# Two attention heads interleaved in hand order: the next head's K work inside the present head's V and gradient work, side work dealt out in slots

## The chip, the cores and the metric

The kernel runs on one core of a Trainium2 chip. The metric is the device time of one execution, in microseconds (us). Several executions are timed, and runs of a changed kernel are timed next to runs of the kernel before on the same chip. The profile is one execution recorded by the hardware; its span is some 2 us shorter than the time on the metric.

Names of engines: PE is TensorE, the matrix engine (PEld is its loading of weights, which overlaps its products: 385.3 and 337.2 us busy in a span of 565.1). DVE is VectorE, ACT is ScalarE, POOL is GpSimd (here it issues stores), SP is SyncE (here it issues loads). In the timelines below each engine starts its instructions in program order, even where a later one is what another engine waits for (DVE runs w_sb and half of dV before pj while PE stands for pj 1.93 us).

## The reference, cut to what matters

The kernel computes a forward pass and all its gradients: one decoding step of attention (32 heads, 4096 cached keys and values each, head width 128) mixed by a gate with a small MLP.

```python
def _A_ref(x, k_cache, v_cache, wq, wo):           # x: one row of 640
    q = (x @ wq) -> 32 heads of 128
    scores = einsum("bhqd,bhkd->bhqk", q, k_cache) * 128 ** -0.5
    p = softmax(scores)
    o = einsum("bhqk,bhkd->bhqd", p, v_cache)
    return o -> one row of 4096 @ wo
def _B_ref(x, w1, b1, w2): ...                     # Mish MLP, 640 -> 1728 -> 640
out = g * a + (1 - g) * b                          # g = sigmoid((x * gate_w).sum())
# returned: out and, by vjp, the gradients of x, k_cache, v_cache, wq, wo, w1, b1, w2, gate_w
```

The large data are K and V (32 MiB each, read) and dK and dV (32 MiB each, written). For one head, with dO the gradient that arrives at o: dP = V dO, ds = p * (dP - sum(p * dP)), dV = p (outer) dO, dK = ds (outer) q, dq = ds K. All of it is matrix times vector: K and V are transposed on PE only to be multiplied by one vector (in the kernel before the transposes are 223.3 of PE's 385.3 busy us).

## The kernel before: the parts that matter

A head is four functions, called one after the other. Two pieces of a head are used throughout this text: a *chunk* is four 128x128 f32 transposes on PE (two bf16 columns are moved as one f32) and an ACT copy of the result out of PSUM; the *products* of a chunk are eight small matrix products with it.

```python
tr_ps bufs=3; sa_ps bufs=2; sb_ps bufs=2; gr_ps bufs=1      # 3 + 2 + 2 + 1: eight PSUM banks in use
def transposes(src, c): ...   # 4 x nc.tensor.transpose(f32), then nc.scalar.copy  ("chunk")
def products(out, tb, c, vec): ...                            # 8 small matmuls

def head_k(h):                       # scores
    for c in range(NT):              # NT = 4 chunks
        ts.append(transposes(kts[h], c))
        if c: products(S, ts[c - 1], c - 1, ...)
    products(S, ts[NT - 1], NT - 1, ...)
    nc.vector.reduce_max(m32[:], S, axis=AX.X)
def head_v(h):                       # V chunks 0..3 with dP = V dO; between them:
    ...                              # MM: transpose of the maximum -> negM -> e = exp(S - max)
    ...                              # Z: sum of e over partitions -> zs -> rz = 1/zs -> p_bf
def head_o(h):
    outer(dV, st["p"], row, 0, J // 2)                        # DVE, half of dV
    nc.vector.scalar_tensor_tensor(pj[:], in0=DP, ..., accum_out=part[:])
    outer(dV, st["p"], row, J // 2, J)
    for j in range(J): nc.tensor.matmul(O, ...)               # 32 one-column products
    nc.tensor.transpose(PT, part[:]...)                       # PE waits for pj
    ...                                                       # dd, ds, o_all on DVE
def head_d(h):
    for j in range(J): nc.tensor.matmul(DQ, ..., rhs=st["ds"]...)   # PE waits for ds
    outer(dK, ...); nc.scalar.copy(dq_all...); outer(dK, ...)

for h in range(H):
    load_k(h + 3); load_v(h + 3)
    if hh == 2: q += prep_steps(g + 1); load_wo(g + 2); ...   # groups of G = 4 heads
    head_k(h); head_v(h)
    if h > 0: side(q if q and hh > 1 else mq, 1)              # one step of side work
    head_o(h)
    side(q if q and hh > 1 else mq, 1)
    head_d(h)
    if hh == G - 1: q += finish_steps(g)
    side(q if q else mq, 1)
    if hh == G - 2 or g == NG - 1: side(q, 4)                 # a block of four steps
```

"Side work" is the MLP, the preparation of the next group of four heads (its q and dO vectors, from wq and wo) and the finishing of the last group (its part of the output, dwo, dx). A step of it may be several large DVE instructions with a PE product in between.

## Time and profile before

| | before |
|---|---|
| time, median | 566.4 us |
| PE, DVE, ACT busy, share of the span | 68%, 56%, 33% |
| a head, from one score maximum to the next | 16.5 us mean, 13.1 to 25.4 |
| full-clock share of that time | 35% |
| bytes moved, mean rate | 165 MB, 292 GB/s |

The first lines are the page of the profile: the span, the busy times, and of the 40 equal slices the rows of PE, of the clock that PE was granted (tenths of full speed) and of DMA (busy share in tenths), then the engines' shares of the chain of waits that ended last.

```profile
span 565.1 us, 13730 instructions
PE 385.3 (68%) x5916; PEld 337.2 (60%) x5916; DVE 313.6 (56%) x780; ACT 188.2 (33%) x410; POOL 46.4 (8%) x95
...
PE   2899776786668735787667655678668755777840
...
PEclk9956556777777757777757666566677776577655
DMA  7995796699779976698784998669878975763493
...
PE 45%; DVE 36%; ACT 7%; issue 6%; DMA 4%; SPq 1%; ACTq 0%; DVEq 0%
```

No engine is full, PE alternates between full and half-empty slices, and the chain changes hands between PE and DVE. The table of waits says on what (total us, how often, longest):

```profile
DVE m L502 <- PE sA L481: 129.8, 31, 13.6
...
DVE zs L525 <- PE sA L522: 44.6, 32, 1.7
...
PE sB L577 <- DVE ds_bf L565: 36.7, 31, 1.4
...
PE sB L560 <- DVE pj L554: 29.9, 31, 2.0
```

DVE waits for scores (m is the score maximum), PE waits for DVE's gradients (pj, ds). One such place in the timeline (start us, duration us, instruction, in brackets the idle time of the engine before it and what ended it):

```profile
313.57 0.94 PE L559 MATMUL sA<-e_bf,Vn 128*128 128x1 bf16 x32
...
314.47 0.67 DVE L453 TENSOR_SCALAR w_sb<-dh_bc,cols_f 128x1728 bf16<-128x1728 bf16 x1
315.06 1.22 DVE L536 TENSOR_TENSOR dV_sb<-p_bf,qd 128x2048 bf16<-128x2048 bf16 x1
...
316.19 0.18 DVE L554 SCALAR_TENSOR_TENSOR pj<-sB,e_bf 128x32 f32<-128x32 f32 x1
...
316.44 0.48 PE L560 MATMUL sB<-ident_f,part 128*128 128x128 f32 x1 [1.93 <-DVE pj L554]
```

PE has finished the products of this head and stands for 1.93 us, because DVE first does side work (w_sb) and half of dV and only then pj.

The last view of the kernel before is the clock. It is cut into windows of 3.41 us (bounds set on the changes of the clock in the trace: in this trace the clock stands at 0.5 or 1.0, for 3.413 us or a whole multiple of it, up to the last record) and shows only the instructions of the tile `tr`, the f32 transposes; the number in brackets after PE counts those that touch the window, and PEclk is the granted clock in it.

```profile
427.50:430.92 3.42, 1.18 (x8) 0.72 (x8) 1.35 (x3) 1.00 0.95 395
430.92:434.33 3.41, 0.08 (x1) 0.11 (x2) 0.00 (x0) 0.50 0.27 111
434.33:437.74 3.41, 3.30 (x14) 2.54 (x15) 1.47 (x3) 0.50 1.00 336
437.74:441.16 3.42, 2.07 (x16) 1.52 (x14) 2.00 (x4) 1.00 0.99 304
441.16:444.57 3.41, 0.84 (x6) 0.42 (x4) 1.17 (x2) 1.00 1.01 420
444.57:447.98 3.41, 0.57 (x3) 0.67 (x4) 0.00 (x0) 0.50 0.97 396
```

A window with 14 transposes at half clock is followed by one at full clock, that one (16) by another, and the one with 6 by a fall. At half clock one transpose starts 213 ns after the other (median over the trace), at full clock 109 ns.

### The profile page before, as it was taken

To read this page: it belongs to the slowest core of one execution; us is meant where nothing else is said; L and a number is where in the kernel's file an instruction comes from. 1 tells how busy PE (TensorE), PEld (TensorE's weight loads), DVE (VectorE), ACT (ScalarE), POOL (GpSimd) and SP (SyncE) were. 2 spreads that over 40 slices of the span, in tenths; PEclk is the share of its full clock that TensorE was granted. 3 is DMA by queue.
4 is the path that set the end of the run, shared out by engine and by line. 5 is a ranking of instruction groups with operands and counts; after the bars stand their busy time and mean duration, and the time that the engine had idled before them with its cause. 6 is when DMAs were issued, how large, how long until landed. Compare 5 with 4: busy or idle time off the path is not lost.

```text
span 565.1 us, 13730 instructions
## 1 busy us (share of the span) xinstructions
PE 385.3 (68%) x5916; PEld 337.2 (60%) x5916; DVE 313.6 (56%) x780; ACT 188.2 (33%) x410; POOL 46.4 (8%) x95
## 2 busy tenths in 40 slices
PE   2899776786668735787667655678668755777840
PEld 1798765675557634676556645677556644666730
DVE  4221655666556775566449673454645483456574
ACT  2403332343333313353423323334334423334310
POOL 0000000010001000010001100010001000010210
PEclk9956556777777757777757666566677776577655
DMA  7995796699779976698784998669878975763493
GB/s 293 419 382 248 283 377 238 231 382 360 315 243 345 383 275 242 228 373 352 277 297 176 365 381 317 235 230 337 320 280 297 360 300 170 246 248 141 176 403 148
DMA packets 26328, 164.93 MB, mean 292 GB/s; under 512 B 2812, under 2 KB 2812, under 8 KB 10012
## 3 DMA queue, kind: packets, MB, share of 16 engines
q1 hardware_dynamic: 14156, 82.03, 40.3%
q0 software_dynamic: 12112, 82.03, 37.3%
q8 instruction: 46, 0.75, 0.5%
q14 instruction: 14, 0.11, 0.1%
HBM read 82.03 MB, written 82.03 MB: 290 GB/s over the span
## 4 chain that ended last, share of the span: by engine, by line
PE 45%; DVE 36%; ACT 7%; issue 6%; DMA 4%; SPq 1%; ACTq 0%; DVEq 0%
PE tr L472 30%; DVE dV_sb L536 13%; ACT tT L474 6%; DVE dK_sb L536 6%; PE sA L481 4%; DMA w_sb<-in_B_w_dram 4%; DVE junk L253 4%; DVE junk L330 4%; PE h_ps L353 3%; PE sB L577 3%; PE sB L481 2%; DVE junk L414 2%; DVE dj L563 2%; DVE junk L450 1%; DVE ds_bf L565 1%
## 5 line engine op out<-in xcount | busy, mean ns | idle before, releaser
L474 ACT COPY tT<-tr 128x512 f32<-128x512 f32 x256 | 149.0, 586 | 152.9 <-PE tr L472 142.5
L472 PE MATMUL tr<-ident_f,Kn 128*128 128x128 f32 x512 | 127.9, 416 | 0.0
L481 PEld LDWEIGHTS <-tT 128*128 128x128 bf16 x2048 | 82.2, 103 | 65.5 <-ACT tT L474 58.9
L472 PE MATMUL tr<-ident_f,Vn 128*128 128x128 f32 x512 | 95.4, 320 | 0.0
L472 PEld LDWEIGHTS tr<-ident_f,Kn 128*128 128x128 f32 x512 | 94.3, 217 | 1.7 <-issue 1.6
L536 DVE TENSOR_TENSOR dV_sb<-p_bf,qd 128x2048 bf16<-128x2048 bf16 x64 | 78.1, 1221 | 18.5 <-ACT p_bf L530 18.5
L502 DVE TENSOR_REDUCE m<-sA 128x1 f32<-128x32 f32 x32 | 6.1, 192 | 129.8 <-PE sA L481 129.8
L536 DVE TENSOR_TENSOR dK_sb<-ds_bf,qd 128x2048 bf16<-128x2048 bf16 x64 | 75.3, 1217 | 0.0
L472 PEld LDWEIGHTS tr<-ident_f,Vn 128*128 128x128 f32 x512 | 67.3, 164 | 0.0
L577 PEld LDWEIGHTS <-Kn 128*128 128x128 bf16 x1024 | 34.7, 107 | 43.6 <-issue 43.6
L481 PE MATMUL sA<-qd,tT 128*128 128x2 bf16 x1024 | 48.1, 168 | 16.3 <-ACT tT L474 16.1
L481 PE MATMUL sB<-qd,tT 128*128 128x2 bf16 x1024 | 45.4, 165 | 17.7 <-ACT tT L474 17.7
L577 PE MATMUL sB<-ds_bf,Kn 128*128 128x1 bf16 x1024 | 31.8, 165 | 36.7 <-DVE ds_bf L565 36.7
L579 ACT CAST dq_all<-sB 128x1 bf16<-128x1 f32 x32 | 5.2, 162 | 132.5 <-PE sB L577 132.5
L557 POOL DMA_DIRECT2D out_dram<-dV_sb x32 | 17.2, 537 | 374.8 <-DVE dj L563 374.8
L560 PE MATMUL sB<-ident_f,part 128*128 128x128 f32 x32 | 13.8, 431 | 30.0 <-DVE pj L554 29.9
L525 DVE TENSOR_REDUCE zs<-sA 128x1 f32<-128x32 f32 x32 | 6.1, 192 | 44.6 <-PE sA L522 44.6
L559 PE MATMUL sA<-e_bf,Vn 128*128 128x1 bf16 x1024 | 30.2, 163 | 0.0
L253 DVE SCALAR_TENSOR_TENSOR junk<-wo_g,da_bc 128x640 bf16<-128x640 bf16 x32 | 26.3, 822 | 4.8 <-DMA wo_g<-in_A_wo_dram 3.8
L559 PEld LDWEIGHTS <-Vn 128*128 128x128 bf16 x1024 | 28.2, 96 | 0.0
L560 PEld LDWEIGHTS sB<-ident_f,part 128*128 128x128 f32 x32 | 5.3, 167 | 32.8 <-DVE pj L554 32.8
L585 POOL DMA_DIRECT2D out_dram<-dK_sb x31 | 16.5, 532 | 102.0 <-DVE dK_sb L536 60.4
(144 smaller groups left out, 332.1 us busy)
## 6 DMA issues: line engine op xcount, KB each, us to landing
Kn<-in_A_k_cache_dram SPq DMA_DIRECT2D x32, 1024.0 KB, 10.0
Vn<-in_A_v_cache_dram SPq DMA_DIRECT2D x32, 1024.0 KB, 12.7
out_dram<-dV_sb POOLq DMA_DIRECT2D x32, 1024.0 KB, 5.0
out_dram<-dK_sb POOLq DMA_DIRECT2D x31, 1024.0 KB, 10.4
wq_g<-in_A_wq_dram SPq DMA_DIRECT2D x4, 1280.0 KB, 7.9
wo_g<-in_A_wo_dram SPq DMA_DIRECT2D x8, 640.0 KB, 13.2
out_dram<-wo_g POOLq DMA_DIRECT2D x8, 640.0 KB, 10.9
out_dram<-dwq_t POOLq DMA_DIRECT2D x5, 896.0 KB, 7.9
```

Of the source, the lines that this page charges most:

```text
L253: nc.vector.scalar_tensor_tensor(junk[:, 0:D], in0=wos[g][:, i, :], scalar=1.0, in1=da_bc[:], op0=ALU.mult, op1=ALU.mult, accum_out=gp["do ...
L330: nc.vector.scalar_tensor_tensor(junk[:], in0=wqs[w][:, rc, :], scalar=1.0, in1=dq_bc[:, w * WG * Dh:(w + 1) * WG * Dh], op0=ALU.mult, op1 ...
L353: nc.tensor.matmul(hps["t"][:, fc:fc + 1], lhsT=w1_sb[:, rc, :].rearrange("p (q c) -> p q c", c=FCN)[:, :, fc], rhs=x_bf[:, rc:rc + 1], st ...
L472: nc.tensor.transpose(tp[:, t, :], flat[:, k * P:(k + 1) * P], ident_f[:])
L474: nc.scalar.copy(sb[:].rearrange("p a b -> p (a b)"), tp[:].rearrange("p a b -> p (a b)"))
L481: nc.tensor.matmul(out[:, 2 * k:2 * k + 2], lhsT=tb[:, t, par, :], rhs=vec[:, par, :], start=(par == 0), stop=(par == 1))
L536: nc.vector.tensor_tensor(dst[:, a:b, :].rearrange("p j (a b) -> p j a b", b=2), col[:, a:b, :].unsqueeze(2).to_broadcast([P, n, Dh // 2, 2]),
L557: nc.gpsimd.dma_start(dVv[h], dV[:])
L559: nc.tensor.matmul(O, lhsT=vts[h][:, j, :], rhs=st["e"][:, j:j + 1], start=(j == 0), stop=(j == J - 1))
L560: nc.tensor.transpose(PT, part[:].to_broadcast([P, P]), ident_f[:])
L577: nc.tensor.matmul(DQ, lhsT=kts[h][:, j, :], rhs=st["ds"][:, j, 0:1], start=(j == 0), stop=(j == J - 1))
L585: nc.gpsimd.dma_start(dKv[h], dK[:])
```

## The change

Its intent: fill PE's waits with the next head's K work, fill DVE's waits with the previous head's dK, and deal the side work out evenly. It adds no arithmetic and moves no other bytes. The core of the diff:

```diff
-    sb_ps = ... bufs=2        gr_ps = ... bufs=1
+    sb_ps = ... bufs=1        gr_ps = ... bufs=2
+    def slot(h, p=2, d=1):    # deals ready items: all "T" (tiny), d of "D" (DVE), p of "P" (PE)
+        ...                   # an item is ready when its deps were dealt in an earlier slot
-    def head_k / head_v / head_o / head_d
+    def period(h):            # K chunks of h+1 live inside head h
+        nc.vector.reduce_max(m32[:], S, axis=AX.X)
+        V(0); dk_half(h - 1, 0)                    # dK of the head before, on DVE
+        V(1); ...MM...; dk_half(h - 1, 1)
+        V(2); dP(0); ...e...; V(3); dP(1); ...Z, zs, rz, p_bf...
+        dP(2); o_part(0, J); dP(3)
+        slot(h)
+        ...pj...                                   # now ahead of dV
+        dv_half(h, 0)
+        nc.tensor.transpose(PT, part...)
+        k_chunk(h + 1, 0, tk); k_chunk(h + 1, 1, tk)
+        ...dd, ds...
+        dv_half(h, 1)
+        s_chunk(h + 1, 0, tk); k_chunk(h + 1, 2, tk)
+        slot(h)
+        s_chunk(h + 1, 1, tk)
+        ...DQ: 32 one-column products...
+        k_chunk(h + 1, 3, tk); s_chunk(h + 1, 2, tk)
+        ...dq copy...
+        s_chunk(h + 1, 3, tk)
+        slot(h)
     for h in range(H):
-        if hh == 2: q += prep_steps(g + 1); load_wo(g + 2); load_wq(...)
+        if hh == 0: prep_steps(g + 1, h)           # now a period earlier: S of the next group
+        if hh == 3: load_wo(g + 2); load_wq(...)   # starts inside period 3; loads a head later
```

`k_chunk` makes a chunk of K, `s_chunk` its products (written S0 to S3 below, the chunks K0 to K3, V0 to V3). The steps of side work were cut into items, most of them of one to four DVE instructions.

## The prediction

> **What bounds the kernel now.** No engine: on the page PE is 68% busy, DVE 56%, ACT 33%, and the DMA queues take 78% of 16 engines' span. From head 0's score maximum (21.0 us, timeline) to head 31's (534.0 us) a head takes 16.5 us (13.1 to 25.4). The chain of waits alternates between PE transposes (30%) and DVE outer products and side work (dV 13%, dK 6%, wq/wo/w1 reductions some 13%), one waiting for the other. In "who waited for whom" DVE waits 129.8 us for scores and 44.6 us for the softmax sum; PE waits behind pj and ds (30 + 37 us), and at heads 11, 19, 27 some 10 us for a block of DVE side work.

> **Clock.** [...] steps of 3.41 us between 0.5 and 1.0 (mean 0.68). [...] windows full of 1-column products stay at half clock; nearly every rise follows a half-clock window with 11 to 13 of the 128x128 f32 transposes. Now K and V lie back to back (32 transposes in 8 to 10 us), which always offers such a window.

> **What the change does.** It removes no arithmetic and no bytes. It puts the next head's K chunks on PE where PE waited for pj, dd, ds; the previous head's dK on DVE where DVE waited for scores and softmax; and deals one DVE item (0.8 to 1.3 us) and up to two PE items per slot, three slots a head, so no 5 to 10 us blocks remain. One sB bank goes to side work; sB is read last by the small dq copy, so one should not stall.

> **Cost of a head after** (timeline durations). PE at half clock: 8 x 1.15 (chunk and product) + O 1.0 + DQ 1.0 + max, sum and part transposes 0.9 + S3 waiting for its copy 0.6 + side 45/32 = 1.4: 14.1; at full clock some 10 to 11 us. DVE: 2.44 + 2.35 + 2.1 small operations + 2.9 side = 9.8 us. ACT 5.9. DMA: 165 MB at 375 to 385 GB/s of its full windows = 435 us, 13.5 us a head. So PE becomes the bound, DMA close behind at about 90%.

> The interleave spreads the transposes: V in one run of 16, K broken by slots and DQ. I expect fewer windows to reach the threshold and the mean clock to *fall* to 0.55 to 0.65, giving back part of the gain: about 14.1 us a head instead of 11 to 12.

> **Sum.** 21 us start + 31 x 14.1 = 437 + 31 tail (534 to 565 before; five dx, dwo and dwq_l still follow the last head) = 489 us. Range 462 to 518. Faster by over 2%: 0.96; within 2%: 0.03; slower: 0.01.

> **What would show it.** Score maxima lie some 14 us apart, evenly; PE busy 83 to 92%, its microseconds somewhat up, clock 0.55 to 0.65; DVE busy 62 to 66%, same microseconds; mean HBM rate 330 to 345 GB/s; in the chain PE over 65%, DVE under 20%, mostly at the ends; waits for scores under 60 us.

> **What would make it wrong.** Faster (near 465): transposes still raise the clock, period near 12.5, then DMA is the floor. Slower (over 515): in-order engines bind each other (negM waits for MM behind V0, V1; pj for the last dP behind O; dV1 stands before slot work), DVE becoming co-critical; or full DMA delays output buffers and loads, showing as DMA waits in the chain.

What the Clock paragraph says is of the trace of the kernel before: from 28.2 to 38.4 us PE is busy with one-column products all the time (10.2 us) at a clock of 0.5; 30 of the 31 rises (first and last five windows left out) follow a half-clock window in which 11 to 13 transposes start, the other one with 14; and the 32 transposes of a head take 7.7 to 9.7 us and put 12 to 14 into one window in 32 of 32 heads. "The threshold" is that count: 30 of 32 half-clock windows with twelve or more are followed by full clock, 1 of 5 with ten or eleven, none of 66 with at most nine. The costs of a head are estimates from durations in the same trace (at half clock a chunk starts 1.15 us after the last, O takes 0.94 us and DQ 0.99, S3 waits 0.54 for its copy; with a transpose every 109 ns in place of 213 the same sum gives 10.8 us, the "10 to 11" at full clock), and so is the floor of DMA: stretches of 17 us with DMA 98% busy or more moved 368 to 386 GB/s.

## The result, and the profile after

The changed kernel takes 464.1 us (462.8 to 465.8, four runs) against 566.4 us. Ratios in this text are the mean time of one kernel's fast runs over the mean of the fast runs of the kernel before in the same rounds, so not quite the ratio of the medians quoted (and where two experiments ran on different chips, the ratios are what can be compared): here 0.820, with a 95% interval of 0.816 to 0.824. The result is correct.

| | before | after |
|---|---|---|
| first score maximum | 21.0 us | 20.7 us |
| a head, mean | 16.5 us | 13.1 us |
| of it PE busy / PE idle | 11.86 / 4.69 us | 11.98 / 1.14 us |
| full-clock share | 35% | 20% |
| last score maximum to the end | 31.1 us | 34.6 us |

(PE busy here is the union of products and weight loads between the first and the last score maximum, over 31 heads.) The same lines of the page as before:

```profile
span 462.1 us, 13671 instructions
PE 389.3 (84%) x5916; PEld 363.1 (79%) x5916; DVE 311.1 (67%) x785; ACT 186.3 (40%) x410; POOL 49.3 (11%) x95
...
PE   2799999999999999799988999799898999999600
...
PEclk9965555656556665687565656656656756556555
DMA  7999999958798899999999899997999999845995
...
PE 61%; DMA 18%; DVE 9%; ACT 7%; issue 2%; SPq 0%; ACTq 0%; DVEq 0%
```

PE's microseconds stayed (385 to 389), the idle time between them went. The clock row lies lower than before (mean 0.61 in place of 0.68). The table of waits, the lines that answer to those before, and two that are new:

```profile
DVE m L621 <- PE sA L559: 42.4, 24, 5.4
...
DVE zs L637 <- PE sA L635: 21.6, 29, 1.2
...
PE sB L651 <- DVE pj L648: 8.5, 16, 2.8
...
DVE junk L278 <- DMA wo_g<-in_A_wo_dram: 8.0, 3, 3.6
...
PE qc_ps L268 <- DMA wq_g<-in_A_wq_dram: 5.7, 3, 2.6
...
PE sB L670 <- DVE ds_bf L659: 1.2, 1, 1.2
```

PE's waits for pj and ds fell from 66.6 to 9.7 us. The waits for wq are new and those for wo have grown (before: one of 3.8 us, at the start), and they weigh more in the chain (DMA 18%) than their 14 us suggest, since the chain then counts the whole transfer that ended last. In the timeline such a place looks so:

```profile
294.75 1.22 DVE L574 TENSOR_TENSOR dV_sb<-p_bf,qd 128x2048 bf16<-128x2048 bf16 x1
296.32 0.61 PEld L268 LDWEIGHTS <-wq_g 128*128 128x128 bf16 x20 [2.37 <-DMA wq_g<-in_A_wq_dram]
```

The clock windows after, in the same view of `tr`:

```profile
303.04:306.46 3.42, 2.07 (x9) 1.81 (x9) 1.17 (x2) 0.50 1.00 419
306.46:309.87 3.41, 2.16 (x9) 1.39 (x8) 1.76 (x3) 0.50 0.98 394
309.87:313.28 3.41, 2.07 (x9) 1.90 (x10) 0.76 (x2) 0.50 0.73 298
313.28:316.70 3.42, 2.04 (x8) 1.25 (x8) 1.38 (x3) 0.50 0.58 230
316.70:320.11 3.41, 2.89 (x12) 2.44 (x12) 1.37 (x3) 0.50 0.98 293
320.11:323.52 3.41, 0.78 (x6) 0.56 (x6) 1.17 (x2) 1.00 0.99 378
```

Here 8 or 9 transposes lie in most windows and the clock stays at half; it rises once, after the window with 12, and the full-clock window is then spent on other work (6 transposes touch it). PE is hardly idle (0.9 us in the four windows before the one with 12): the spread of the transposes, not idleness, seems to keep the clock down. That was the forecast; the experiments test it.

### The profile page after: what moved, and what is told of

The parts are those of the page before. It is cut to its first block, busy times and chain, and to the rows that moved or that the text cites. A ratio compares the mean times of both kernels' runs of the same rounds, so it can differ in the third digit from the quotient of the medians.

```text
span 462.1 us, 13671 instructions
## 1 busy us (share of the span) xinstructions
PE 389.3 (84%) x5916; PEld 363.1 (79%) x5916; DVE 311.1 (67%) x785; ACT 186.3 (40%) x410; POOL 49.3 (11%) x95
## 4 chain that ended last, share of the span: by engine, by line
PE 61%; DMA 18%; DVE 9%; ACT 7%; issue 2%; SPq 0%; ACTq 0%; DVEq 0%
PE tr L550 35%; DMA wo_g<-in_A_wo_dram 10%; DMA wq_g<-in_A_wq_dram 8%; ACT tT L552 5%; PE sB L670 5%; PE sA L559 5%; PE h_ps L404 3%; PE sA L618 3%; PE sB L559 2%; DVE junk L375 2%; DVE junk L278 2%; PE sB L651 2%; PE sA L625 1%; DVE zs L637 1%; PE ap_ps L356 1%
## 5 line engine op out<-in xcount | busy, mean ns | idle before, releaser
L550 PE MATMUL tr<-ident_f,Kn 128*128 128x128 f32 x512 | 121.8, 400 | 0.0
L550 PE MATMUL tr<-ident_f,Vn 128*128 128x128 f32 x512 | 119.9, 396 | 0.0
L559 PEld LDWEIGHTS <-tT 128*128 128x128 bf16 x2048 | 90.1, 107 | 36.6 <-ACT tT L552 29.5
L550 PEld LDWEIGHTS tr<-ident_f,Vn 128*128 128x128 f32 x512 | 93.3, 209 | 0.0
L550 PEld LDWEIGHTS tr<-ident_f,Kn 128*128 128x128 f32 x512 | 91.7, 207 | 0.3 <-issue 0.3
L574 DVE TENSOR_TENSOR dK_sb<-ds_bf,qd 128x2048 bf16<-128x2048 bf16 x64 | 77.7, 1216 | 0.0
L618 PEld LDWEIGHTS <-Vn 128*128 128x128 bf16 x1024 | 31.2, 100 | 5.0 <-issue 5.0
L670 PEld LDWEIGHTS <-Kn 128*128 128x128 bf16 x1024 | 29.7, 103 | 2.0 <-issue 2.0
L627 DVE TENSOR_REDUCE negM<-sA 128x1 f32<-128x128 f32 x32 | 9.3, 291 | 25.6 <-PE sA L625 25.6
L375 DVE SCALAR_TENSOR_TENSOR junk<-wq_g,dq_bc 128x1024 bf16<-128x1024 bf16 x20 | 24.3, 1216 | 0.1
L637 DVE TENSOR_REDUCE zs<-sA 128x1 f32<-128x32 f32 x32 | 6.1, 192 | 21.9 <-PE sA L635 21.6
```

Source lines behind the costliest of these rows:

```text
L375: nc.vector.scalar_tensor_tensor(junk[:], in0=wqs[w][:, rc, :], scalar=1.0, in1=dq_bc[:, w * WG * Dh:(w + 1) * WG * Dh], op0=ALU.mult, op1 ...
L550: nc.tensor.transpose(tp[:, t, :], flat[:, k * P:(k + 1) * P], ident_f[:])
L559: nc.tensor.matmul(out[:, 2 * k:2 * k + 2], lhsT=tb[:, t, par, :], rhs=vec[:, par, :], start=(par == 0), stop=(par == 1))
L574: nc.vector.tensor_tensor(dst[:, a:b, :].rearrange("p j (a b) -> p j a b", b=2), col[:, a:b, :].unsqueeze(2).to_broadcast([P, n, Dh // 2, 2]),
L618: nc.tensor.matmul(O, lhsT=vts[h][:, j, :], rhs=st["e"][:, j:j + 1], start=(j == 0), stop=(j == J - 1))
L670: nc.tensor.matmul(DQ, lhsT=kts[h][:, j, :], rhs=ds[:, j, 0:1], start=(j == 0), stop=(j == J - 1))
```

## The experiments

Eleven kernels ran, in three rounds or more. Their first purpose is to divide the gain; the second, to test the clock, the DMA and the late loads.

### e1 and e2: which part made the gain

e1 keeps the even dealing and takes the interleave and the deferral of dK back:

```diff
-        V(0); dk_half(h - 1, 0) ... dk_half(h - 1, 1)
-        (K chunks of h+1 between PT and the last slot)
+        slot(h); DQ; dk_half(h, 0); dq copy; dk_half(h, 1); slot(h)
+        for c in range(NT): k_chunk(h + 1, c, tk); if c: s_chunk(h + 1, c - 1, tk)
+        s_chunk(h + 1, NT - 1, tk)
```

> Changed kernel, but the K work of the next head stands after DQ in one run and dK follows its own head, as before; side work still dealt in slots. If the even dealing is most of the gain: under 510 us, DVE waits for the scores still large. If the interleave of K is most of it: over 520 us. Clock theory (transposes in one run of 32 raise the clock): mean clock back to 0.66 or more, from 0.61; PE busy under 75%.

e2 keeps the interleaved period and takes side work, its order and the PSUM banks from the kernel before:

```diff
-        slot(h)                  # three times
+        side_at(h, 1..3)         # the side() calls of the kernel before, at the same three places
-    sb_ps bufs=1, gr_ps bufs=2
+    sb_ps bufs=2, gr_ps bufs=1
```

> The head of the changed kernel (K interleaved, dK one head later), with the side work, its order and the PSUM banks of the kernel before. If the interleave is most of the gain: under 510 us; if the dealing is: over 520 us. Heads at group ends should still be several us longer than the others (20 us or more against 12 to 13). Clock 0.58 to 0.64.

Measured: e1 513.5 us (ratio 0.907), e2 498.9 us (0.877; one of its four runs, the profiled one, is slow and left out of the ratio). e1 fell between its two alternatives, e2 within its first: by the ratios, dealing alone saves 53 us, the interleaved period alone (K's interleave and the deferral of dK, not separated here) 70 us, both together 102 us. They overlap by some 20 us, since both remove the same PE idle time: PE idles 4.69 us a head before, 2.59 in e1, 2.06 in e2 and 1.14 after. e2's heads are uneven as expected (10.3 to 23.7 us). The figures inside e2 are from its slow run, which had the clock (0.597) of a fast one that took 499.3 us.

One expectation of e1 was plainly missed: the clock did not return to 0.66, it was 0.639, although K and V lay back to back again. The trace shows how. In its later part e1's heads take 13.6 us one after the other, which is four windows of 3.41 us, so heads keep their place against the windows; in this position the run of 32 gives 8, 8 and 13 transposes, only the third raises the clock, and the window that gets it has 3 or 4. So nearly every head still wins its full-clock window, but only when its transposes are over. A long run alone is no guarantee; where it lies against the windows counts too. (PE was 77% busy, over the 75% expected.)

A kernel with the old banks in the changed kernel could not be run: a deadlock. The dealt items hold a side bank from one slot to the next (o4 is computed in one, copied in a later one), so one bank is likely too few; the second side bank seems a condition of the dealing. What it is worth by itself stays open.

### e3: the late loads

```diff
-        if hh == 0 and g + 1 < NG:
+        if hh == 1 and g + 1 < NG:      # prepare the next group one head later
```

> Changed kernel with the preparation of the next group dealt one head later, so that the wq and wo loads have a head more to land. If the late loads hold PE up as the four holes near 190, 242, 293 and 347 us suggest: 454 to 458 us, no wait on DMA for wq_g or wo_g in the table of waits after the start. If full DMA only moves the wait to other loads: 461 to 465 us.

Measured: 453.3 us (0.798; six runs, one slow and left out of the ratio), just under its first range, and the waits went as forecast. The waits of PE for wq_g fell from 5.7 to 0.8 us, after the start none for wo_g is left; idle PE fell from 1.14 to 0.88 us a head. Changing one number makes it better than the changed kernel by 11 us. Some 8 us (31 x 0.26) are PE's idle time; the rest is not divided. The profiled run of e3 is its fastest, 14.8 us below the changed kernel's, and has a clock of 0.63; over the fast runs the clock is 0.604 to 0.628, against 0.610 to 0.619 for the changed kernel, so a better clock is not shown.

### e4: is DMA close behind PE?

```diff
-            nc.gpsimd.dma_start(dVv[h], st["dV"][:])
+            nc.gpsimd.dma_start(dVv[h][:, 0:J // 2, :], st["dV"][:, 0:J // 2, :])   # wrong result
```

> Wrong result on purpose: only half of each dV is stored, 16.8 of 165 MB less. If PE bounds the heads: 2% less at most, 455 to 463 us, mostly from loads that land sooner. If DMA bounds them: 8 to 10% less, under 430 us.

Measured: 456.5 us (0.805). A tenth fewer bytes saves 1.8% (0.805 over 0.820; 1.6% by the medians), as the first alternative has it, and PE's idle time, 0.86 us a head in place of 1.14, makes as much as all of it (31 x 0.28 = 8.7 us): again the loads that land sooner. So the number of bytes does not bound the changed kernel; late loads cost it some 8 us.

### e5, e6 and e8: the clock

e5 builds on e3 and puts the K work in one piece. Nothing is added or removed:

```diff
         s_chunk(h + 1, 0, tk); k_chunk(h + 1, 2, tk)
-        slot(h)
         s_chunk(h + 1, 1, tk)
-        DQ
         k_chunk(h + 1, 3, tk); s_chunk(h + 1, 2, tk)
+        slot(h)
+        DQ
         dq copy
         s_chunk(h + 1, 3, tk)
```

> e3 with the K work in one piece: K0 K1 S0 K2 S1 K3 S2, then the slot and DQ, then S3, so that DQ and not idle PE covers S3's wait for its copy (0.6 us a head, 19 us in all), and 16 K transposes stand together. If PE alone bounds the heads: 434 to 442 us. If DMA or DVE is as close as PE: 448 us or more. Clock theory (a window needs some 12 transposes): mean clock at or above e3's 0.63.

("Some 12" is what the trace of the kernel before shows: 30 of 32 half-clock windows with twelve or more transposes are followed by full clock; over all traces, pooled below, 287 of 302, but also 54 of 164 with ten or eleven.)

Measured: 427.1 us (0.751; one slow run left out of the ratio), outside both alternatives, on the fast side. The clock is 0.72, the full-clock share of the heads 43% in place of 24%, PE busy 10.88 us a head in place of 11.87 in e3. The view of `tr`:

```profile
226.49:229.90 3.41, 3.29 (x14) 2.54 (x15) 1.46 (x3) 0.50 1.01 418
229.90:233.31 3.41, 2.10 (x16) 1.58 (x15) 1.80 (x4) 1.00 1.01 421
233.31:236.73 3.42, 0.64 (x4) 0.41 (x4) 1.24 (x3) 1.00 1.02 421
236.73:240.14 3.41, 1.14 (x6) 1.34 (x7) 0.04 (x1) 0.50 1.00 423
```

But e5 changes two things: the run of transposes, and DQ now covers S3's wait for its copy. e8 separates them. It is e5 with the 32 one-column products of O, which nothing waits for soon, moved into the K work:

```diff
-        dP(2); o_part(0, J); dP(3)
+        dP(2); dP(3)
 ...
         s_chunk(h + 1, 0, tk)
+        o_part(0, J)
         k_chunk(h + 1, 2, tk)
```

> e5 with one thing moved: the 32 one-column products of O stand between the K transposes (after S0) instead of between dP2 and dP3, so K is broken into 8 and 8 transposes, while S3's wait stays covered by DQ. If the unbroken run is what raised the clock in e5: clock back to 0.60 to 0.66, 438 to 448 us. If the covered S3 wait was the gain, or the clock follows busy PE: clock 0.70 or more, 424 to 430 us.

Measured: 449.3 us (0.794), just over its first range, with the clock in it: 0.64, full-clock share 25%. Same instructions, same cover for S3, and breaking the run of 16 into 8 and 8 costs 22 us (24 by the ratios; the two ran on different chips). In the view of `tr`:

```profile
297.43:300.85 3.42, 1.91 (x8) 1.71 (x8) 1.14 (x2) 0.50 1.00 418
300.85:304.26 3.41, 2.19 (x8) 1.43 (x8) 1.10 (x3) 0.50 1.02 426
304.26:307.67 3.41, 2.32 (x10) 2.24 (x11) 1.02 (x3) 0.50 1.02 404
307.67:311.09 3.42, 1.24 (x10) 0.87 (x9) 1.44 (x3) 1.00 0.96 393
```

But the move has a second effect: O had covered two other waits, which lie open in e8, while e5 alone waits long for wq. From the tables of waits, two lines of e8 and one of e5:

```profile
PE sB L650 <- DVE pj L647: 18.4, 29, 1.8
PE sB L559 <- ACT tT L552: 6.5, 21, 0.3
```

```profile
PE qc_ps L268 <- DMA wq_g<-in_A_wq_dram: 19.8, 3, 10.7
```

(In e5 the wait for pj is 6.8 us; in e8 that for wq is 0.7.) So the total time of e8 does not separate the two, and neither does its small distance from e3 (0.794 against 0.798, intervals that overlap). PE's busy time does, since the instructions are the same: 11.87 us a head in e3, 11.78 in e8, 10.88 in e5. What the higher clock is worth is therefore 31 x 0.90 = 28 us from e8 to e5 and 31 x 0.99 = 31 us from e3 to e5. The covered wait of S3 was worth something too (PE's waits before S products are 19.2 us in e3 and 1.9 in e5), but the wait for wq took as much back: idle PE is 0.88 us a head in e3, 0.91 in e8 and 1.09 in e5. So what e5 gains over e3 is PE's busy time at the higher clock; the idle time, taken together, rose. The rival, that the clock follows how busy PE is, falls too: PE is 86% busy in e8 at 0.64 and 83% in e5 at 0.72.

e6 goes further: DQ of a head moves into the next head's period, so that K of the next head and its V stand in one run of 32.

```diff
         dP(3)
+        dq(h - 1, A[:, 96:97])        # DQ of the head before, into a free column of this head's bank
         slot(h)
 ...
-        DQ and dq copy of h at the end of the period
-        slot(h) ... slot(h)           # the second and third slot
+        slot(h, 1) ... slot(h, 0)     # deal fewer PE items
```

> e3 with the DQ products of a head moved into the next head's period, between the last dP and the part transpose, so that the K transposes of the next head and its V transposes stand in one run of 32, as in the kernel before. Clock theory: mean clock 0.68 or more, two full-clock windows in four, PE time of a head from 11.9 to 11 us or less. If that carries through: 420 to 432 us; if DMA or DVE becomes the bound: 435 to 450 us with the clock up all the same. Rival, that the clock follows how busy PE is: the clock stays at 0.63.

Measured: 440.6 us (0.775; the profiled run is slow). The clock rose as forecast, to 0.72 to 0.73 in the three fast runs, but the time is not in the range for a gain that carries through, only in the second one (435 to 450 us), and worse than e5. DVE waits 29.3 us for the part transpose, which now stands behind DQ (22.3 us in e5, of which 10.5 are one wait for wq), and the last head has an unshared DQ at the end (40.2 us from the last score maximum to the end). Which of these costs more, or whether it is the smaller slots, was not tested, and these profile numbers are from a slow run.

Pooled over the traces of the two kernels and all eleven experiments, counting the transposes that start in each window and leaving out the first and last five windows of a trace (a few windows before the first record of the clock are taken as half): of 683 half-clock windows with at most nine, 4 are followed by full clock; of 164 with ten or eleven, 54; of 302 with twelve or more, 287. Among full-clock windows the same number divides: 110 of 114 with twelve or more keep it, 7 of 328 with at most nine. (In the traces of the two kernels alone: 45 of 48 half-clock windows with twelve or more are followed by full clock, 6 of 23 with ten or eleven, 1 of 133 with at most nine; of full-clock windows 25 of 27 with twelve or more keep it, none of 47 with at most nine.) At half clock twelve transposes fill 12 x 213 ns = 2.6 us of a window's 3.41, at full clock 12 x 109 ns = 1.3 us. By these figures full clock takes half as much of a window's time to keep as to win. Nor is it idleness that keeps the clock down: of 200 half-clock windows in which PE or its weight loads are busy for over 3.35 us and at most nine transposes start, 4 are followed by full clock.

Those 4 say that the transposes need not be the cause as such: three of them hold 7 or 8 transposes and 18 products of 96 columns of the MLP (e4, e7, e8), the fourth (changed kernel, at 350.8 us) 9 and four bf16 products of 128 columns. A count of all wide products would take in these four too, but 1024 of the 1215 recorded products of 96 columns or more are the transposes (both kernels), and no experiment separates the two.

### e7: was deferring dK worth it?

```diff
-        V(0); dk_half(h - 1, 0) ... dk_half(h - 1, 1)
         (o_all)
+        dk_half(h, 0); dk_half(h, 1)
```

> Changed kernel with dK computed right after its own head's dV instead of under the next head's V work. If the deferral matters because DVE would hold up the next score maximum: 475 to 490 us, DVE idle in V work, wait of MM for the maximum in the table. If DVE has slack there: 462 to 470 us.

Measured: 476.7 us (0.840), 12.6 us slower than the changed kernel, so the deferral matters. The profile agrees with the first alternative only in part: dK appears on the chain of waits (6%), and DVE does idle during V (its waits for zs are 59.1 us, for negM 46.0 us, after: 21.6 and 25.6), but no wait of MM for the maximum appears among the longest.

### e9, e10 and e11: what bounds e5

e10 is e5 with half of each dV stored, the edit of e4 again:

> Wrong result on purpose: e5 with only half of each dV stored, 16.8 of 165 MB less. The same cut took 1.6% from the changed kernel. If e5 has moved the bound to DMA: 5 to 9% less than e5, 390 to 406 us. If PE still bounds it: 418 us or more.

Measured: 404.5 us (0.713), 5.1% less than e5 (0.713 over 0.751). The same cut that took 1.8% from the changed kernel takes 5.1% here, within the range for DMA (390 to 406 us), though half of the bytes' share (10%). The trace shows where: of the 22 us that the heads gain, 17 lie in the two heads that waited for wq (19.4 to 11.1 us, 24.7 to 15.7), and 22 of the other 29 take the same time to within 0.5 us. So DMA bounds e5 through loads that come late, not in every head. The DMA lines of e5's slices show no room for them: busy nine tenths or more almost throughout, and 417 to 425 GB/s in 13 of the 20 slices of the second half:

```profile
DMA  7999999995999999999999999999999999989992
GB/s 257 420 405 356 422 423 422 413 386 183 382 344 409 413 381 424 407 406 309 420 423 420 423 425 424 418 417 378 363 421 423 423 424 422 422 341 405 404 404 79
```

e5 still had two heads of 19.4 and 24.7 us, held up by the wq load. e9 and e11 reorder the loads:

```diff
 e9:  +   if hh == 3: load_wo(g + 2); load_wq(...)      # moved ahead of
          load_k(h + 3); load_v(h + 3)
 e11: +   if hh == 3: load_wq(...)                      # only wq ahead; wo stays behind K and V
```

> e5 with the wo and wq loads of a group put ahead of that head's K and V loads in the load queue. The heads of 19.4 and 24.7 us in e5 held PE up to 10.8 us for wq. If it is the place in the queue: holes under 4 us, 415 to 421 us. If DMA is full anyway and bounds the kernel: the hole is paid elsewhere, 424 us or more.

> e5 with only the wq load ahead of that head's K and V loads and the wo load left behind them, because in e9 the load queue stood still from 234 to 252 us behind a wo load that waited for its buffer. If that blocking is what e9 paid: no head above 16 us after the first seven, 414 to 420 us. If DMA, full either way, sets the time: 421 to 428 us as e5 and e9.

Measured: e9 423.3 us (0.750, interval 0.745 to 0.755), e11 425.1 us (0.752, 0.746 to 0.758), e5 427.1 us (0.751, 0.747 to 0.756). The three cannot be told apart. In e9 PE waited at most 8.4 us for wq (10.7 in e5) and one head still took 23.9 us: the load queue stood from 235 to 252 us, with a wo load at its head that waited 17.8 us for its buffer (the store of wo_g); the wq, K and V loads behind it started only after it, at 253.2 to 255.0 us. e11 has no such wait for wq (0.8 us), but one head of 26.6 us, in which DVE waits 12.5 us for wo: its hope for no head above 16 us failed. With DMA full (share 1.00 to 1.03 in e9 from 225 to 285 us, 417 to 428 GB/s), a better order of loads moved the wait. e5, e9 and e11 beat both kernels and are correct.

## Why the prediction was right

**Direction and range: right, near the edge.** Predicted 489 us (462 to 518), measured 464.1, faster by far more than 2%. The measured time is the one that the prediction named for being wrong on the fast side ("near 465": the transposes still raise the clock, and DMA is the floor). That is not what happened: the clock fell as forecast and e4 shows no floor of DMA. That the range still held 464 owes something to its width; where the 25 us went is the sum of several terms, below.

**Bound before (PE and DVE waiting for each other): right.** PE idled 4.69 us a head before and 1.14 after, while its busy time stayed; that is 31 x 3.55 = 110 us against the 102 us gained (the tail is 3.5 us longer).

**The clock falls: right, and tested.** Forecast 0.55 to 0.65, measured 0.61 to 0.62. The step "windows full of 1-column products stay at half clock" holds: in the kernel before from 28.2 to 38.4 us (PE busy 10.2 us, clock 0.5), and over all traces in 196 of 200 half-clock windows with PE busy and at most nine transposes, the other 4 with wide products in them. e5 against e8 shows that the unbroken run raises the clock (0.72 against 0.64). "Nearly every rise follows a half-clock window with 11 to 13" transposes is a little narrower than the traces show: 54 of 164 windows with ten or eleven and those 4 with at most nine were followed by full clock too. e1 shows that a run of 32 that offers such a window is not enough: in its later heads the window with 13 comes last, and the full clock it wins falls on other work.

**Head cost: mechanism right, size off.** The forecast said 14.1 us a head, the trace 13.12. Its terms, with what they measured (a straight line fitted over the 31 heads of the trace gives the head's own PE time as 11.72 us at half clock, less 0.25 us for each us at full clock):

| term of the sum | predicted | measured |
|---|---|---|
| head's own PE work at half clock | 9.2 + 1.0 + 1.0 + 0.9 = 12.1 | 11.72 |
| full clock part of the time | nothing | -0.25 x 2.61 = -0.65 |
| PE side work | 1.4 | 0.92 |
| PE waiting | 0.6 (S3) | 1.14 |
| sum | 14.1 | 13.13 |

The step that failed is "about 14.1 us a head instead of 11 to 12": it priced a head wholly at half clock, while the same text forecast a mean clock of 0.55 to 0.65, and it took side work from the kernel before, where it was computed as engine time shared out over heads, not as time that PE was busy with nothing else. The error is 31 x 0.97 = 30 us; a tail 3.6 us longer than forecast gives a little back.

**Evenly spaced heads: half right.** The 24 us heads are gone, but the range is 10.5 to 18.2 us. The longest are the early heads with 4.5 to 5.3 us of PE side work (15 products of the MLP's first layer, 2.7 us an item), then those that wait for wq.

**The chain: DVE right, PE too high, DMA missed.** DVE has 9% (forecast under 20), PE 61 (over 65). The 18% of DMA were not in the forecast, which names DMA waits in the chain only as a way to be slower: the change prepares the next group of heads two heads sooner and loads its weights one head later, so that their lead shrinks from four heads to one, and I did not follow that through. e3 prices it at 11 us.

**"DMA close behind at about 90%": right in rank, wrong in capacity.** e4 (1.8% for a tenth of the bytes) shows that DMA does not bound the changed kernel, whose PE is 84% busy. But the capacity was taken as 375 to 385 GB/s from full windows of the kernel before; e5 holds 420 to 425. The floor of 435 us that followed from it was too high: e9 runs at 423 us. The mean rate was forecast at 330 to 345 GB/s and is 357, and DVE's share at 62 to 66% and is 67, both since the time is shorter.

**"One should not stall" (one sB bank):** nothing in the waits speaks against it, but no run isolates it.
